# Pacing a batch's loads on the compute of an earlier batch, in a banded attention with a SiLU feed-forward layer

## The chip, the cores and the metric

The kernel runs on one core of a Trainium2 chip. The metric is device time in microseconds (us) of one execution. Lower is better.

## The reference

The kernel computes attention in a causal window of 64 positions, then two dense layers with SiLU between them. Cut to what matters:

```python
# q, k, v: (8 batches, 8 heads, 576 positions, 64), float32
rel = pos[:, None] - pos[None, :]
mask = (rel >= 0) & (rel < 64)
scores = where(mask, (q @ k.T) / sqrt(64), -1e9)
attn = softmax(scores)
x = (attn @ v).transpose(0, 2, 1, 3).reshape(8 * 576, 512)
h = x @ w_in                       # w_in: 512 x 2048
out = (h * sigmoid(h)) @ w_out     # w_out: 2048 x 512, float32 out: 4608 x 512
```

## The kernel before

**The work.** Attention goes by batch: eight of them, each with nine blocks of 64 positions. From batch 2 on, a batch is done in three groups g of three blocks; a group's scores are 24 small matmuls (`scores`, L353), followed by four exponentials on ScalarE (`expo`, L367), four mask products on VectorE (`masking`, L370), 24 matmuls with V (`values`, L376), two reciprocals of the row sums (`inverse`, L383) and two products that normalise (`normal`, L389). The result of a group is turned and written to the tile `bridge`: by TensorE (L393, L404) in the early groups, and by a DMA transpose that SyncE issues (`turn_o`, L398) from the last group of batch 2 on.

The dense part goes by tiles of 512 rows, nine of them, numbered j from 0. A tile's first layer is 64 matmuls (`first_layer`, L409) with 16 SiLUs (L415); its second layer is four times 16 matmuls (`second_layer`, L418), each sixteen copied out of PSUM (`copy_out`, L424, on VectorE or ScalarE) and stored by SyncE (`store`, L428). A tile can begin when the groups of attention that its rows come from are in `bridge`. The attention of later batches is put between the second-layer matmuls of earlier tiles.

**The loads.** Q, K and V of a batch are loaded and cast to bf16 by DMAs that GpSimd issues. From batch 4 on for Q (2 for K), a batch's Q and K come in 16 loads (`load_rows`, L262) into four of the eight buffers `nat0` to `nat7`; each buffer holds two pairs of heads, filled by four loads. Then one DMA transpose for each buffer, issued by SyncE (`turn_rows`, L268), writes it into `qt` or `kt`, of which there are two each, used by batches in turn. So a batch has four such transposes: Q and K of its first half, then Q and K of its second half. V comes in four loads (`load_v`, L276) into one of three buffers `vv`, and two copies on VectorE (`shift_v`, L336 and L338) shift it into place.

**The order.** Each engine runs its instructions in the order in which they were written out. That order comes from a planner in the kernel's own code (`Plan.run`), which walks through time with an estimated cost for each operation (the number in `{"POOL": 0.72}` and the like) and an estimated delay for each DMA, and gives a free engine the ready operation of the highest rank. The estimates decide the order alone; on the chip an instruction starts when its engine gets to it and the semaphores of the data it needs have been raised. GpSimd's loads also wait each for the landing of the load eight before it, as eight semaphores are used in turn; SyncE's DMAs do the same.

Around the change: in the planner, the loads of a batch b from 2 on are held until a planned time, by

```python
hold = {b: p.later(31.0 * b - 31.0 * LEAD) for b in range(2, B)}   # LEAD = 1.5
...
[nat_free.get(i)], dma=0.5, gate=late(b), lat=MARGIN
```

This hold exists in the planner's clock only. On the chip nothing holds the loads but their buffers (`nat_free`: the buffer's last transpose; for V the last use of `vv`) and the eight semaphores.

Of the kernel before, what the change touches and what calls it, by code (L numbers as in the profile page):

```python
# [14 lines left out]
class Plan:  # L15
# [5 lines left out]
    def __init__(self, pools, rank, rank0, ahead):  # L21
        self.rank, self.rank0, self.pools = rank, {**rank0, **{c + "0": r for c, r in ahead.items()}}, pools
        self.queues = {}
        self.banks = [[] for _ in range(8)]
        self.count, self.times = 0, []
        self.now = 0.0

    def add(self, cls, us, fn, deps=(), lat=0.08, gate=None, dma=None, pool=None, table=None, b=0, nb=1):
# [4 lines left out]
        self.count += 1  # L33
        self.queues.setdefault(cls, []).append(op)
        return op

    def later(self, us):
        self.times.append(us)
        return lambda: self.now >= us

    def add_filler(self, n, cls, us, fn, *args, **kw):

# [8 lines left out]
    def run(self):  # L51
        head = {c: 0 for c in self.queues}
        engines = sorted({e for q in self.queues.values() for op in q for e in op["us"]})
        free = {e: 0.0 for e in engines}
        can = {e: [c for c, q in self.queues.items() if any(e in op["us"] for op in q)] for e in engines}
        table, left = "exp", self.count
        pipe, sent = {True: 1.8, False: 0.0}, []
        events, order = [0.0, *self.times], []
        while left:
            if not events:  # L60
                raise RuntimeError([(c, head[c], q[head[c]]["n"]) for c, q in self.queues.items() if head[c] < len(q)])
            now = self.now = heapq.heappop(events)
            while events and events[0] == now:
                heapq.heappop(events)
            moved = True
            while moved:
                moved = False
                for e in engines:
                    if free[e] > now:
                        continue  # L70
                    best, kept = None, set()
                    heads = [(self.queues[c][head[c]], c) for c in can[e] if head[c] < len(self.queues[c])]
                    for op, c in sorted(heads, key=lambda x: x[0]["first"]):
                        if e == "POOL" and op["dma"] and len(sent) >= 8 and sent[-8] > now:
                            continue
                        if e not in op["us"] or not self.done(op["deps"]) or (op["gate"] and not op["gate"]()):
                            continue
                        if op["pool"]:
                            idle = [i for i in self.pools[op["pool"]] if i not in kept and self.done(self.banks[i])]
                            if len(idle) < len(op["untils"]):  # L80
                                if op["pool"] != "mp":
                                    kept.update(self.pools[op["pool"]])
                                continue
                            idle.sort(key=lambda i: (op["pool"] == "mp" and i in self.pools["pv"],
                                                     max([u["seen"] for u in self.banks[i]], default=0.0)))
                            op["bank"] = idle[:len(op["untils"])]
                            for i, until in zip(op["bank"], op["untils"]):
                                self.banks[i] = until
                        best = (op, c)
                        break  # L90
                    if best is None:
                        continue
                    op, c = best
                    head[c] += 1
                    us = op["us"][e]
                    if op["table"] and op["table"] != table:
                        table, us = op["table"], us + 1.28
                    end = free[e] = now + us
                    soft = e == "POOL"
                    if op["dma"] is None:  # L100
                        op["seen"] = end + op["lat"]
                    elif soft:

                        begin = max(pipe[True], end + 1.4)
                        pipe[True] = begin + op["dma"] * (1.5 if pipe[False] > begin else 1.0)
                        op["seen"] = pipe[True] + op["lat"] + (1.2 if now < 40 else 3.2)
                        sent.append(op["seen"])
                        heapq.heappush(events, op["seen"])
                    else:
                        begin = max(pipe[False], end + 1.0)  # L110
                        busy = pipe[True] > begin
                        pipe[False] = begin + op["dma"] * (1.6 if busy else 1.0)
                        if busy:
                            pipe[True] += 0.6 * op["dma"]
                        op["seen"] = pipe[False] + {"ld0": 1.2, "st": 1.2}.get(c, 3.0)
                    op["at"], op["cls"], op["by"] = now, c, e
                    order.append((op, e))
                    left -= c != "warm"
                    moved = True
                    heapq.heappush(events, end)  # L120
                    heapq.heappush(events, op["seen"])
        for op, e in order:
            op["fn"](e)
# [3 lines left out]
def kernel(ctx, tc, q, k, v, w_in, w_out, out):  # L127
# [18 lines left out]
    NXQ, NXK, NXO = 4, 2, 3  # L146
    NOX, NRC, NV = 4, 6, 3
    NIV = 2
    NM0, LEAD, MARGIN = 9, 1.5, 1.3
    scale = 1.0 / float(D) ** 0.5  # L150


# [4 lines left out]

    ident = keep.tile([128, 128], BF16, name="ident")
    zero = keep.tile([128, NP], FP32, name="zero")
    spare = keep.tile([128, NP], FP32, name="spare")  # L160
    window = keep.tile([128, 64], BF16, name="window")
    mask0 = keep.tile([128, 2, 3, 64], BF16, name="mask0")
# [269 lines left out]
    v_landed = {}  # L432
    kq_done, v_done, s_last, pv_last = {}, {}, {}, {}
    nat_free, natb_free = {}, {}
    g_pv, g_norm, g_back, g_mask, o_done = [], [], [], [], {}
    moe = []
    exps = {}

# [9 lines left out]
    scores_may_run.i = 0  # L448

    n_nat = [0, 0]  # L450
    hold = {b: p.later(31.0 * b - 31.0 * LEAD) for b in range(2, B)}

    def late(b):
        return hold.get(b)

    def add_first_batch():
        got = {}
        for what, u in FIRST_LOADS:
# [32 lines left out]
    def add_batch_qk(b):  # L491
        pool = "mp" if b == 3 else "at"
        slot, parts = {}, {0: [], 1: []}
        for pj in range(NP):
            kq_done[(b, pj)] = []
        for pj in range(NP):
            busy = s_last.get((b - NK, pj), []) + ([c_k[b % NK]] if b < NK else [])
            for kk in range(2):
                if b >= (NXK if kk else NXQ):
                    if pj % 2 == 0:  # L500
                        slot[kk] = n_nat[0] % NN
                        n_nat[0] += 1
                    i = slot[kk]
                    parts[kk] += [p.add("dma", {"POOL": 0.72}, lambda _, i=i, pj=pj, kk=kk, hh=hh: load_rows(i, b, pj, kk, hh),
                                        [nat_free.get(i)], dma=0.5, gate=late(b), lat=MARGIN) for hh in range(2)]
                    if pj % 2 == 0:
                        continue
                    both = busy + s_last.get((b - NK, pj - 1), [])
                    done = [p.add("xk", {"SP": 1.4}, lambda _, i=i, pj=pj, kk=kk: turn_rows(i, place(b, pj - 1, kk)),
                                  parts[kk] + both, dma=2.2)]  # L510
                    nat_free[i] = done[0]
                    parts[kk] = []
                    for x in (pj - 1, pj):
                        kq_done[(b, x)] += done
                    continue
                w = n_nat[1] % NNB
                n_nat[1] += 1
                ca = [p.add("dma", {"POOL": 0.66}, lambda _, w=w, pj=pj, kk=kk: load_cast(w, b, pj, kk),
                            [natb_free.get(w)], dma=0.65, gate=late(b), lat=MARGIN)]
                tu = p.add("turn", {"PE": 0.27}, None, ca + [c_ident], lat=0.1, pool=pool, b=b)  # L520
                tu["fn"] = lambda _, tu=tu, w=w: turn_twos(tu, w)
                li = []
# [10 lines left out]

    def add_v_loads(b, parts, busy):
        v_landed.setdefault(b, []).extend(
            p.add("dma", {"POOL": 1.0}, lambda e, part=part: load_v(e, b, part), busy, dma=1.1, gate=late(b), lat=MARGIN * (b > 0)) for part in parts)

    def add_batch_v(b):
        busy = pv_last.get(b - NV, []) + [c_vv[b % NV]]
# [9 lines left out]
    def add_batch_attention(b):  # L549
        pv_last[b] = []  # L550
        whole = b > 1
        for g, a in [(g, a) for a in range(2) for g in range(NG)] if b == 0 else [(g, a) for g in range(NG) for a in range(1 if whole else 2)]:
            add_unit(b, g, range(2) if whole else [a], len(g_pv))

    def add_unit(b, g, which, n0):
# [38 lines left out]
        for i, (n, a) in enumerate(zip(ns, which)):  # L594
            rc = p.add("inverse" + first, {"DVE": 0.21}, lambda _, i=i, n=n: inverse(pv["bank"][i], n),
                       [pv] + g_norm[n - NRC:n - NRC + 1] * (n >= NRC), b=b)
            was = n // 2 - NOX
            no = p.add("norm" + first, {"DVE": 0.56}, lambda e, i=i, n=n: normal(e, pv["bank"][i], n),
                       [rc] + (g_back[2 * was:2 * was + 2] if was >= 0 else []), b=b)
# [128 lines left out]
```

## Time and profile before

| | |
|---|---|
| median of 13 runs | 312.89 us |
| lowest, highest | 309.11, 315.83 us |
| the profiled execution | 314.45 us |
| its span, first to last instruction | 312.7 us |
| TensorE (PE) busy | 296.9 us, 95% |
| ScalarE (ACT), GpSimd (POOL), VectorE (DVE) busy | 185.0, 117.7, 102.2 us |
| first batch-4 load, first batch-5, -6, -7 load issued | 70.14, 89.86, 112.88, 138.35 us |
| last load issued | 160.30 us |
| K or Q transposes, issue to landing | 3.3 to 11.8 us, median 9.1 (K) and 8.7 (Q) |

How to read what follows: the profile is one execution. Engines are PE (TensorE matmuls), PEld (its weight loads), DVE, ACT, POOL and SP (SyncE); a q after the name (SPq) is the engine's sequencer, which issues DMAs and waits. "out<-in" gives the tiles written and read, with buffer numbers left out. Times are microseconds from the start of the span. The "chain" is the work that ended last, followed back step by step to what released it: its rows are start, duration, what. In a timeline a row is start, duration, engine, line, operation, tiles, count, and in brackets the idle time of the engine before it with what ended that.

### The profile page before, as it was taken

The numbers are of one execution on the slowest core, as the hardware profiler recorded it, in microseconds if no ns is written. First come the engines' busy times: TensorE is split into PE (matmuls) and PEld (weight loads), VectorE is DVE, ScalarE is ACT, GpSimd is POOL, SyncE is SP. The second block draws the span as 40 slices with busy tenths as digits, with TensorE's granted clock in tenths as the row PEclk, the third lists the DMA queues.
The fourth block names the chain that finished last, engine by engine and source line by source line (L and its number), as shares of the span: only waits on it lengthen the run. The fifth ranks groups of instructions, "written<-read, shape, count | busy, mean of one in ns | idle before, by whom it ended". The sixth has DMA issues, their size and how long they took to land.

```text
span 312.7 us, 6586 instructions
## 1 busy us (share of the span) xinstructions
PE 296.9 (95%) x2645; PEld 147.6 (47%) x2675; DVE 102.2 (33%) x273; ACT 185.0 (59%) x340; POOL 117.7 (38%) x159
## 2 busy tenths in 40 slices
PE   4999989999999999995999999999999999999995
PEld 2565445445454455442454455445444444444444
DVE  2573877725682066204361056103301200000000
ACT  4788986879466762874328742855478156316611
POOL 8957859866896482773760000000000000000000
PEclk9999999999999999998699999999999999999999
DMA  8999999999999999999999607901400410010012
GB/s 171 162 197 186 193 194 145 186 208 148 189 144 168 120 169 168 157 175 126 171 145 195 101 36 179 150 0 69 107 11 2 93 69 1 34 68 35 0 67 69
DMA packets 137599, 37.57 MB, mean 120 GB/s; under 512 B 122464, under 2 KB 132832, under 8 KB 137568
## 3 DMA queue, kind: packets, MB, share of 16 engines
q0 software_dynamic: 95328, 18.06, 78.8%
q1 hardware_dynamic: 42240, 19.08, 32.7%
q8 instruction: 21, 0.34, 0.5%
q14 instruction: 10, 0.08, 0.1%
HBM read 36.70 MB, written 9.44 MB: 148 GB/s over the span
## 4 chain that ended last, share of the span: by engine, by line
PE 86%; DMA 5%; DVE 3%; issue 2%; ACT 2%; POOL 1%; SPq 0%; POOLq 0%; ACTq 0%
PE mp L409 38%; PE mp L418 37%; DMA kt<-nat 3%; PE mp L376 3%; PE at L353 3%; DMA nat<-in_k_dram 2%; ACT g L415 1%; PE at L313 1%; PE at L303 1%; PE at L376 1%; PE at L673 1%; DVE kt L322 1%; POOL natb L249 1%; PE mp L673 1%; PE at L393 0%
## 5 line engine op out<-in xcount | busy, mean ns | idle before, releaser
L418 PE MATMUL mp<-w_out_sb,g 128*128 128x512 bf16 (+2 forms) x578 | 132.2, 373 | 3.1 <-issue 2.1
L409 PE MATMUL mp<-bridge,w_in_sb 128*128 128x512 bf16 (+2 forms) x600 | 129.4, 370 | 0.3
L415 ACT ACTIVATE g<-mp 128x512 bf16<-128x512 f32 (+2 forms) x150 | 85.3, 580 | 30.1 <-PE mp L409 28.9
L409 PEld LDWEIGHTS <-w_in_sb 128*128 128x128 bf16 x600 | 57.3, 97 | 66.1 <-issue 6.0
L418 PEld LDWEIGHTS <-g 128*128 128x128 bf16 x608 | 55.9, 99 | 59.5 <-issue 3.3
L367 ACT ACTIVATE e<-at 128x384 bf16<-128x384 f32 x88 | 36.8, 496 | 25.1 <-PE at L353 24.6
L424 ACT COPY ot<-mp 128x512 f32<-128x512 f32 (+2 forms) x28 | 15.5, 556 | 58.4 <-PE mp L418 44.9
L370 DVE TENSOR_TENSOR e<-e,mask 128x384 bf16<-128x384 bf16 x84 | 27.0, 353 | 68.8 <-ACT e L367 68.2
L262 POOL DMA_DIRECT2D nat<-in_k_dram x48 | 35.6, 745 | 19.5 <-DMA nat<-in_k_dram 10.1
L276 POOL DMA_DIRECT2D vv<-in_v_dram x32 | 32.1, 1011 | 5.3 <-DMA natb<-in_q_dram 1.5
L262 POOL DMA_DIRECT2D nat<-in_q_dram x32 | 23.7, 745 | 9.4 <-DMA vv<-in_v_dram 5.4
L389 DVE TENSOR_TENSOR ox<-mp,rc 128x384 bf16<-128x384 f32 x37 | 18.5, 537 | 0.0
L376 PEld LDWEIGHTS <-e 128*64 128x64 bf16 x576 | 11.5, 110 | 10.3 <-issue 8.3
L353 PE MATMUL at<-qt,kt 64*128 64x64 bf16 x528 | 13.1, 192 | 3.5 <-DMA kt<-nat 3.3
L353 PEld LDWEIGHTS <-kt 64*128 64x128 bf16 x576 | 10.2, 95 | 11.6 <-issue 7.2
L383 DVE RECIPROCAL rc<-mp 128x6 f32<-128x6 f32 x37 | 7.0, 195 | 21.5 <-PE mp L376 21.4
L424 DVE COPY ot<-mp 128x512 f32<-128x512 f32 x10 | 6.8, 691 | 20.5 <-PE mp L418 19.2
L376 PE MATMUL mp<-vv,e 128*64 128x65 bf16 x444 | 10.8, 196 | 0.2
L322 DVE COPY qt<-at 64x288 bf16<-64x288 bf16 x16 | 7.7, 479 | 7.5 <-ACT qt L322 7.1
L243 POOL DMA_DIRECT2D natb<-in_q_dram x12 | 7.9, 657 | 4.8 <-PE at L313 1.2
L338 DVE COPY vv<-vv 64x576 bf16<-64x576 bf16 (+1 forms) x14 | 8.0, 568 | 3.6 <-issue 2.1
L367 ACT ACT_TABLE_LOAD x7 | 9.0, 1283 | 0.1
(62 smaller groups left out, 137.8 us busy)
## 6 DMA issues: line engine op xcount, KB each, us to landing
out_dram<-ot SPq DMA_DIRECT2D x35, 256.0 KB, 3.7
vv<-in_v_dram POOLq DMA_DIRECT2D x32, 144.0 KB, 7.7
nat<-in_k_dram POOLq DMA_DIRECT2D x48, 72.0 KB, 7.5
nat<-in_q_dram POOLq DMA_DIRECT2D x32, 72.0 KB, 8.4
natb<-in_q_dram POOLq DMA_DIRECT2D x15, 144.0 KB, 6.1
w_in_sb<-in_moe_w_in_dram POOLq DMA_DIRECT2D x8, 256.0 KB, 8.3
w_out_sb<-in_moe_w_out_dram POOLq DMA_DIRECT2D x8, 256.0 KB, 7.4
natb<-in_k_dram POOLq DMA_DIRECT2D x7, 144.0 KB, 5.9
```

Of the source, the lines that this page charges most:

```text
L262: nc.gpsimd.dma_start(out=rows(i)[:, pj % 2, :, 64 * hh:64 * hh + 64], in_=(q, k)[kk][b, head(pj, hh)].rearrange("(m p) d -> p m d", p=NR),)
L276: queue[e].dma_start(out=vv[b % NV][:, 2 * g0 + 1:2 * g1 + 1:2, 0:D], in_=v[b].rearrange("h s d -> (h s) d").rearrange("(g p) d -> p g d", ...
L322: copies[e](out=place_one(b, pj, kk)[64 * hh:64 * hh + 64].rearrange("x (p m) -> x p m", m=NM)[:, :, r::2], in_=at_bf16(op)[64 * r:64 * r ...
L353: nc.tensor.matmul(at_six(of[hh])[:, j, x], lhsT=kt[b % NK][r, at:at + 128], rhs=qt[b % NK][r, at:at + 64], start=(b > 0 and j == x == 0), ...
L367: nc.scalar.activation(out=es[n % NE], in_=at_six(bank), func=ACTF.Exp, scale=scale)
L370: nc.vector.tensor_mul(es[n % NE], es[n % NE], mask0 if g == 0 else mask)
L376: nc.tensor.matmul(at_pv(bank)[64 * hh:64 * hh + 64, j, x], lhsT=es[(2 * n + hh) % NE][:, j, x], rhs=vv[b % NV][:, head(2 * a + j, hh) * N ...
L389: nc.vector.tensor_mul(ox(n), at_pv(bank)[:, :, :, 0:D], rcs[n % NRC].unsqueeze(3).to_broadcast([128, 2, 3, D]))
L409: nc.tensor.matmul(banks[bank["bank"][0]][:, lo:hi], lhsT=w_in_sb[:, c, ft * 128:(ft + 1) * 128], rhs=bridge[:, (j * TT + lo) // 64:(j * T ...
L415: nc.scalar.activation(out=gts[gt][:, lo:hi], in_=banks[bank["bank"][0]][:, lo:hi], func=ACTF.Silu)
L418: nc.tensor.matmul(banks[bank["bank"][0]][:, 0:hi - lo], lhsT=gts[gt][:, m * 128:(m + 1) * 128], rhs=w_out_sb[:, f, lo:hi], start=(f == 0) ...
L424: copies[e](out=ots[ot][:, lo:hi], in_=banks[bank["bank"][0]][:, 0:hi - lo])
```

## The change

The planner's hold goes. In its place the loads of each batch b from 4 on wait on the chip: ahead of them GpSimd runs a copy of one column of the first reciprocal of batch b - 2 into a tile `pace` that nothing reads. GpSimd takes its instructions in order, so all the loads after the copy wait for that reciprocal. The planner sees the copy and its dependency like any other operation.

```diff
-    def later(self, us):
-        self.times.append(us)
-        return lambda: self.now >= us
...
-    NM0, LEAD, MARGIN = 9, 1.5, 1.3
+    NM0, MARGIN, PACED, BEHIND = 9, 1.3, 4, 2
...
+    pace = keep.tile([128, 1], FP32, name="pace")
...
-    hold = {b: p.later(31.0 * b - 31.0 * LEAD) for b in range(2, B)}
-
-    def late(b):
-        return hold.get(b)
...
     def add_batch_qk(b):
         pool = "mp" if b == 3 else "at"
         slot, parts = {}, {0: [], 1: []}
+        if b >= PACED:
+            n = first_unit[b - BEHIND]
+            p.add("dma", {"POOL": 0.15}, lambda _: nc.gpsimd.tensor_copy(out=pace, in_=rcs[n % NRC][:, 0, 0:1]), [g_inverse[n]])
...
-                                        [nat_free.get(i)], dma=0.5, gate=late(b), lat=MARGIN) for hh in range(2)]
+                                        [nat_free.get(i)], dma=0.5, lat=MARGIN) for hh in range(2)]
...
     def add_batch_attention(b):
         pv_last[b] = []
         whole = b > 1
+        first_unit[b] = len(g_pv)
...
             rc = p.add("inverse" + first, {"DVE": 0.21}, lambda _, i=i, n=n: inverse(pv["bank"][i], n),
                        [pv] + g_norm[n - NRC:n - NRC + 1] * (n >= NRC), b=b)
+            g_inverse.append(rc)
```

(`gate=late(b)` goes in the same way from the cast loads and from `load_v`.)

As the planner now sees other load times, it writes out another order. In the built programs:

- GpSimd: the same order, with one copy ahead of the 16 Q/K loads of batches 4, 5, 6 and 7.
- TensorE: the same until the first layer of tile 4. Then batch 6's scores begin at once instead of after 12 second-layer matmuls of tile 4; batch 7's first group moves from tile 5 to tile 4, its second and third groups from tiles 5 and 6 to tile 5.
- VectorE: the two V shifts of batch 4 move from behind batch 3's first group to behind the masks of its second and third group; those of batch 7 move from behind batch 6's third group to behind the masks of its second and third. Four copies out of PSUM move to ScalarE, which has two table loads fewer.
- SyncE: from batch 4 on, as this table shows (Qn.h and Kn.h: transposes of batch n, half h; On.g: turned output of batch n, group g; S: a store).

| | SyncE's order |
|---|---|
| before | O2.2, Q4.0, S, K4.0, O3.0, Q4.1, K4.1, S, O3.1, S, O3.2, O4.0, S, Q5.0, K5.0, S, O4.1, Q5.1, K5.1, S, O4.2, S, O5.0, Q6.0, S, O5.1, K6.0, S, O5.2, Q6.1, K6.1, S, S, O6.0, Q7.0, S, O6.1, K7.0, S, O6.2, Q7.1, K7.1 |
| after | O2.2, S, Q4.0, O3.0, K4.0, Q4.1, K4.1, S, O3.1, S, Q5.0, O3.2, K5.0, O4.0, S, S, O4.1, Q5.1, K5.1, Q6.0, K6.0, S, O4.2, S, Q6.1, O5.0, K6.1, O5.1, S, S, O5.2, Q7.0, K7.0, Q7.1, K7.1, S, O6.0 |

## Prediction

> **What bounds the kernel now.** I read the first part of the page, then the chain of waits between 134 and 165 us, TensorE's timeline there, the stretches with their granted clock, and last the DMA issues and SyncE's timeline.
>
> ```profile
> span 312.7 us, 6586 instructions
> PE 296.9 (95%) x2645; PEld 147.6 (47%) x2675; DVE 102.2 (33%) x273; ACT 185.0 (59%) x340; POOL 117.7 (38%) x159
> ...
> DMA  8999999999999999999999607901400410010012
> ```
>
> TensorE is the bound: 95% busy. A change gains only where TensorE stands idle or runs at a lower clock. The DMA engines are full until about 172 us (22 slices of 7.8 us), while TensorE needs its last batch only at 212 us.
>
> ```profile
> 136.39 0.67 SPq L268
> ...
> 137.26 10.50 DMA kt<-nat
> 147.76 0.05 issue
> 147.81 0.50 PE at L353 x9
> 148.31 0.34 issue
> 148.65 5.23 PE mp L418 x12
> ...
> 154.99 2.75 PE mp L418 x12
> ```
>
> This is the one place after 50 us where the chain leaves TensorE for long: the last K transpose of batch 5, issued by SyncE at 137.26, lands 10.50 us later. TensorE's timeline has the same stop (a row in brackets gives the idle time and who ended it), and the stretches show what follows it:
>
> ```profile
> 144.15 0.35 PE L353 MATMUL at<-qt,kt 64*128 64x64 bf16 x12
> 147.81 0.50 PE L353 MATMUL at<-qt,kt 64*128 64x64 bf16 x12 [3.31 <-DMA kt<-nat]
> ```
> ```profile
> 145.00:146.80 1.80, 0.00 (x0) 0.00 (x0) 0.92 (x3) 0.40 (x2) 0.00 (x0) 1.00 2.02 59
> 146.80:148.00 1.20, 0.19 (x8) 0.19 (x10) 0.00 (x0) 0.00 (x0) 0.19 (x1) 0.51 3.20 109
> 148.00:153.60 5.60, 5.26 (x24) 1.95 (x19) 0.72 (x2) 0.87 (x2) 4.26 (x7) 0.50 2.21 172
> ```
>
> The seventh number column, ahead of DMA share and GB/s, is the granted clock: 1.00 until 146.8, then 0.50 until 153.6. So the stop costs 3.31 us of idle, 0.18 us more issue time (0.34 against 0.16 at the next switch) and 2.48 us of half clock (12 recorded matmuls in 5.23 us against 2.75). Sum 5.97 us. The half clock begins 2.3 us after the idle time does (144.50 to 146.8).
>
> Why did that transpose come so late? Its loads were issued by 108.1 us (GpSimd's timeline) and landed by 115.3. It stood in SyncE's queue:
>
> ```profile
> 103.95 5.30 SPq L268 DMA_TRANSPOSE kt<-nat  x1
> ...
> 116.11 0.34 SPq L428 DMA_DIRECT2D out_dram<-ot  x1
> 117.11 5.08 SPq L398 DMA_TRANSPOSE bridge<-ox  x2
> 122.28 0.56 SPq L428 DMA_DIRECT2D out_dram<-ot  x1
> 123.05 3.88 SPq L268 DMA_TRANSPOSE qt<-nat  x1
> 127.11 3.33 SPq L268 DMA_TRANSPOSE kt<-nat  x1
> ```
>
> Batch 5's first Q transpose, with its data there since about 103 us, waits behind turned outputs and a store that wait for compute. Each transpose then takes long beside loads. Three K transposes, issued at 103.95, 137.26 and 193.22 us, by the DMA issues of windows that hold just these (last number: us to landing):
>
> ```profile
> kt<-nat SPq DMA_TRANSPOSE x1, 11.3
> ```
> ```profile
> kt<-nat SPq DMA_TRANSPOSE x1, 10.5
> ```
> ```profile
> kt<-nat SPq DMA_TRANSPOSE x1, 3.3
> ```
>
> The third ran when no load was left. The first is batch 4's last: it landed at 115.23, and TensorE's scores of batch 4 began at 115.85, their second half at about 116.1. That is a margin of 0.9 us.
>
> **The four copies.** A copy of 128x1 on GpSimd is not in the trace; the nearest GpSimd rows are a 128x1 memset (0.09 us) and a 128x128 select (0.29 us). Four cost 0.4 to 1.2 us of GpSimd, an engine 38% busy and off the chain; they cannot gain by themselves. I take 0.2 each, beside TensorE's work. What they cost is the wait. Behind each stand, on GpSimd, all 20 loads of its batch and of every later one; for them wait SyncE's transposes, for these the scores.
>
> **When the loads now run.** Batch 4: before from 70.14; now after the first reciprocal of batch 2 (VectorE, 82.97 plus 0.2) and the copy: 83.4. Its 16 Q/K loads took 15.4 us before and take 11.6 if nothing but the issue time counts (16 times 0.725); I take 13, as few transposes run beside them: until 96.4. V adds 4.2: 100.6. Batch 5: the reciprocal of batch 3 is done at 92.9, so the copy waits for nothing; loads start at 100.6 (before 89.86), at the old 18.2 + 4.3 us until 123.1. Batch 6: reciprocal of batch 4 at 119.8, also past; 123.1 (before 112.88), 20.2 + 4.2, until 147.5. Batch 7: reciprocal of batch 5, 154.23 less the gain, about 149: a wait of some 1.5 us, then 19.0 + 4.0, until 172. So the loads run 10 to 13 us later, and only batch 4's wait is a real one.
>
> **The queue order.** Until batch 5's scores TensorE's order is unchanged; SyncE's is not. Batch 4: a store and one turned output now stand ahead of its transposes. The store's copy ends at 92.8 (92.10 + 0.69), so the store goes by 93.5 and the first Q transpose at 93.5 instead of 91.10; its loads (the sixth issued at about 87.4, landing in 5) are there. With the old durations (2.75, 3.01, 2.17, 3.12 and four gaps of 0.15) the last K transpose starts at 105.2, against 103.95; the sixteenth load, issued by 96.4 and landing in 5.6 to 9.6, is there by then. Landing after 11.3: 116.5. Needed at 116.1: a wait of 0.4 us. The bounds are a landing 3 us earlier, thus 0, and 2.5 us later, which is past 2.3 us of idle and brings 2.5 us of half clock.
>
> Batch 5: first Q and K move ahead of two turned outputs and two stores. From 116.6 with the old durations: Q 3.88, turned output 1.88, K 3.33, turned output 1.22, two stores 1.1, turned output 2.28, Q 3.40, eight gaps of 0.15: the last K starts at 134.9 instead of 137.26. Loads do not hold it: the sixth lands at about 113.3, the eighth at 117.9, the sixteenth at 126.1 (old times plus 10.8). Plus 10.5 it lands at 145.4; needed at 144.5 plus the 0.4 of batch 4. About 0.7 us of idle remains, too short for the half clock. Bounds: the rows of K transposes beside loads spread from 9.3 to 11.8 us to landing, and one SyncE issue from 2.2 to 5.3: 0 to 3 us, with 2.5 more past 2.3.
>
> Batch 6: two transposes now stand right behind, held until batch 4's last scores (139.4) and their loads (the eighth lands at about 142.6). Behind them waits a store whose copy is ready at 143.7 and a turned output whose norms end at 145.4, needed by a tile that starts 45 us later: nothing.
>
> **The rest of the replan.** The two 0.76 us V shifts of batch 4 on VectorE move behind masks, into idle time shown ahead of reciprocals (0.98 and 1.40): nothing. Four copies out of PSUM move from VectorE to ScalarE (4 times 0.56) while two table loads (1.28 each) go: nothing, as ScalarE is 59% busy; without that cover, one second layer's 3.46 us for 16 matmuls must hold four exponentials (1.64) and a copy (0.59), which it does. Batch 7's first scores come much earlier, at about 186 instead of 212: behind the first layer of tile 4 (172.6) and 13.4 us of other work. Its last K transpose starts at about 173 and lands in 4 to 10: 177 to 183. V lands at 178 to 182, while its shift stands on VectorE at about 181, ahead of a reciprocal and four masks: 0, with 1.5 as the upper bound.
>
> **The sum.** The profiled execution took 314.45 us, 1.75 more than its span, and 1.56 more than the median of 312.89, so the usual stop is likely a shorter one than this one. 314.45 - 5.97 + 0.4 + 0.7 = 309.6 us. Without any wait it is 308.5; the fastest run before was 309.11, so such a floor is near what this kernel already reached.
>
> [...] In the trace 3.31 us of idle were followed by 6.8 us at 0.50. [...] Transposes landed in 10.5 us beside loads and 3.3 without. [...]
>
> **The rivals.**
> *Batch 4 comes late (slower).* Its margin was 0.9 us and its loads start 13 us later. For it: landings of 11.3 us. Against: SyncE's own queue, not the loads, set the old start. It decides when the last K transpose lands after 119.6, that is, starts after 108.3: 3.5 us idle and 2.5 of half clock give back the 5.97, so 314.5, and 315.2 with batch 5's 0.7.
> *No gain.* Batch 5's last transpose still lands over 2.3 us late, as loads crowd it as before. 2.5 idle and 2.5 of clock: 308.5 + 5.0 = 313.5.
> *Real relief.* The late loads leave the transposes room and both waits vanish: 308.5. For it: the 3.3 us row; against: the load queue is dry only from 69.5 to 83.4, before any of these transposes.
> *The change does less than it says:* three of four copies hold nothing. That is in my forecast already.
>
> **How the numbers follow.** About 0.5% (1.6 us) is what a measurement here can tell from no change. Forecast (308.9 to 311.3) 0.47; relief 0.17; no gain (311.3 to 314.45) 0.17; batch 4 late (above that) 0.19. Faster: 0.64, same 0.17, slower 0.19. The range goes from 308.2, just under the floor, to 315.2, the slower rival with both waits.
>
> **What would show it.** Right: GpSimd idle from 69.5 to about 83 and hardly before batches 5 and 6; batch 5's last K transpose issued near 135; no stretch at 0.50 near 147. Wrong: TensorE idle on a transpose at 116, or at 186, or a granted clock of 0.50 anywhere between 60 and 300.

## The result and the profile after

The changed kernel is slower: 320.38 us (median of 11 runs, 316.69 to 322.54) beside 313.15 us for the kernel before on the same chips, a ratio of 1.0227 with a 95% interval of 1.0197 to 1.0256. Medians take in all executions; ratios leave out those that took over 1.5% longer than the fastest of the same kernel. The profiled execution took 322.54 us, the longest of the eleven; its span is 320.4 us.

The page of the changed kernel answers to the one of before:

```profile
span 320.4 us, 6596 instructions
PE 297.0 (93%) x2645; PEld 148.2 (46%) x2675; DVE 99.2 (31%) x269; ACT 184.9 (58%) x342; POOL 118.5 (37%) x163
...
PEclk9999999999999999999999965999999999999999
DMA  8999999999599999999999995200400120020012
```

TensorE's busy time is the same, 297.0 us against 296.9. The extra 7.7 us of span are idle time, and slices 24 and 25 (8 us each) show a fallen clock. Slice 11 of the DMA row, 80 to 88 us, has a hole that was not there before. TensorE's timeline at the stop that the change was forecast to remove, and at the one that came:

```profile
144.20 0.35 PE L350 MATMUL at<-qt,kt 64*128 64x64 bf16 x12
144.96 0.35 PE L350 MATMUL at<-qt,kt 64*128 64x64 bf16 x12 [0.41 <-DMA kt<-nat]
...
181.52 2.97 PE L415 MATMUL mp<-w_out_sb,g 128*128 128x512 bf16 x13 [0.16 <-issue]
194.63 1.35 PE L373 MATMUL mp<-vv,e 128*64 128x65 bf16 x24 [10.15 <-DVE e L367]
195.91 0.82 PE L350 MATMUL at<-qt,kt 64*128 64x64 bf16 x24
197.06 5.39 PE L415 MATMUL mp<-w_out_sb,g 128*128 128x512 bf16 x15 [0.34 <-issue]
```

(Lines here stand three lower than before: L415 is the second layer, L373 the product with V, L367 the mask, L335 one V shift.) Batch 5's stop of 5.97 us is down to 0.41. At 184.5 TensorE then stands still for 10.15 us, and what follows runs slowly. The stretches have the granted clock in the third column from the end:

```profile
184.50:187.40 2.90, 0.00 (x0) 0.00 (x0) 0.00 (x0) 0.00 (x0) 0.00 (x0) 1.00 3.62 121
187.40:194.60 7.20, 0.00 (x0) 0.00 (x0) 2.29 (x7) 0.00 (x0) 0.00 (x0) 0.50 1.44 214
194.60:201.00 6.40, 6.03 (x58) 3.19 (x60) 4.08 (x12) 2.24 (x5) 0.00 (x0) 0.50 0.46 105
```

Against rows of the same kind at full clock (0.57, 0.52, and 2.97 us for 13 matmuls) the work after 194.6 lost 0.8 + 0.3 + 2.0 us, and 0.2 at the switch: 3.2 us. The books close: 312.7 - 5.97 + 0.41 + 10.15 + 3.2 = 320.5, against a span of 320.4.

Who holds TensorE is in the chain of waits:

```profile
152.83 13.00 DMA nat<-in_q_dram
165.83 0.28 issue
166.12 11.45 DMA nat<-in_q_dram
...
181.04 11.11 DMA vv<-in_v_dram
192.15 0.03 issue
192.18 0.05 DVEq L335
...
192.27 0.12 DVE vv L335
...
194.31 0.28 DVE e L367
```

Read backwards: the product with V waits for a mask, the mask stands on VectorE behind a shift of V of batch 7, and that V lands at 192.15. Its last load was issued at 181.04, because loads of batch 7 had waited, through the eight semaphores, for loads that took 13.00 and 11.45 us: the ninth, at 166.12, for the first, which landed at 165.83, and the first V load for the ninth, which landed at 177.56. Before the change, batch 7's first load went out at 138.35 and its last V landed at 171.8; now the first goes out at 152.83, so 14.5 of the 20.3 us come from the later start and the rest from slower loads. The product that stands still belongs to batch 6; it needs nothing of batch 7. Batch 7's last K transpose was no earlier: SyncE issued it at 186.36 and it landed at 192.9.

GpSimd's timeline shows the copies, L488, and the loads behind them:

```profile
83.29 0.18 POOL L488 COPY pace<-rc 128x1 f32<-128x1 f32 x1 [13.93 <-DVE rc L380]
...
100.15 0.22 POOL L488 COPY pace<-rc 128x1 f32<-128x1 f32 x1
...
152.72 0.22 POOL L488 COPY pace<-rc 128x1 f32<-128x1 f32 x1
...
157.88 0.72 POOL L259 DMA_DIRECT2D nat<-in_q_dram  x1 [1.17 <-DMA vv<-in_v_dram]
162.95 0.72 POOL L259 DMA_DIRECT2D nat<-in_k_dram  x1 [4.34 <-DMA vv<-in_v_dram]
```

Only the first copy waited for its reciprocal, 13.93 us. The others ran as soon as GpSimd came to them.

### The profile page after: what moved, and what is told of

Its sections match the earlier page's. It is cut to its first block, busy times and chain, and to the rows that moved or that the text cites. A ratio compares the mean times of both kernels' runs of the same rounds, so it can differ in the third digit from the quotient of the medians.

```text
span 320.4 us, 6596 instructions
## 1 busy us (share of the span) xinstructions
PE 297.0 (93%) x2645; PEld 148.2 (46%) x2675; DVE 99.2 (31%) x269; ACT 184.9 (58%) x342; POOL 118.5 (37%) x163
## 4 chain that ended last, share of the span: by engine, by line
PE 69%; DMA 23%; POOL 3%; issue 3%; DVE 1%; POOLq 0%; SPq 0%; ACT 0%; DVEq 0%; ACTq 0%
PE mp L415 31%; PE mp L406 29%; DMA nat<-in_q_dram 8%; DMA natb<-in_q_dram 5%; DMA vv<-in_v_dram 3%; DMA kt<-nat 3%; DMA w_out_sb<-in_moe_w_out_dram 3%; PE mp L373 2%; PE at L350 2%; POOL vv L273 2%; DMA nat<-in_k_dram 1%; POOL w_out_sb L285 1%; PE at L300 1%; PE at L373 1%; PE mp L670 1%
## 5 line engine op out<-in xcount | busy, mean ns | idle before, releaser
L415 PE MATMUL mp<-w_out_sb,g 128*128 128x512 bf16 (+2 forms) x578 | 131.2, 372 | 3.2 <-issue 2.2
L415 PEld LDWEIGHTS <-g 128*128 128x128 bf16 x608 | 55.8, 99 | 59.4 <-issue 3.2
L421 ACT COPY ot<-mp 128x512 f32<-128x512 f32 (+2 forms) x32 | 17.8, 560 | 62.8 <-PE mp L415 47.4
L367 DVE TENSOR_TENSOR e<-e,mask 128x384 bf16<-128x384 bf16 x84 | 27.1, 353 | 44.9 <-ACT e L364 44.1
L259 POOL DMA_DIRECT2D nat<-in_q_dram x32 | 23.8, 749 | 12.7 <-DMA vv<-in_v_dram 8.4
L373 PEld LDWEIGHTS <-e 128*64 128x64 bf16 x576 | 12.0, 112 | 20.5 <-DVE e L367 11.9
L373 PE MATMUL mp<-vv,e 128*64 128x65 bf16 x444 | 11.6, 199 | 10.3 <-DVE e L367 10.1
L335 DVE COPY vv<-vv 64x576 bf16<-64x576 bf16 (+1 forms) x14 | 8.3, 591 | 36.5 <-DMA vv<-in_v_dram 29.8
L380 DVE RECIPROCAL rc<-mp 128x6 f32<-128x6 f32 x37 | 6.3, 188 | 15.4 <-PE mp L373 13.7
L319 ACT COPY qt<-at 64x288 bf16<-64x288 bf16 x16 | 7.6, 476 | 0.7 <-DVE qt L319 0.2
L310 PEld LDWEIGHTS <-natb 96*128 96x128 bf16 x96 | 5.7, 97 | 4.7 <-issue 1.8
```

Of the source, the lines that this page charges most:

```text
L259: nc.gpsimd.dma_start(out=rows(i)[:, pj % 2, :, 64 * hh:64 * hh + 64], in_=(q, k)[kk][b, head(pj, hh)].rearrange("(m p) d -> p m d", p=NR),)
L319: copies[e](out=place_one(b, pj, kk)[64 * hh:64 * hh + 64].rearrange("x (p m) -> x p m", m=NM)[:, :, r::2], in_=at_bf16(op)[64 * r:64 * r ...
L367: nc.vector.tensor_mul(es[n % NE], es[n % NE], mask0 if g == 0 else mask)
L373: nc.tensor.matmul(at_pv(bank)[64 * hh:64 * hh + 64, j, x], lhsT=es[(2 * n + hh) % NE][:, j, x], rhs=vv[b % NV][:, head(2 * a + j, hh) * N ...
L415: nc.tensor.matmul(banks[bank["bank"][0]][:, 0:hi - lo], lhsT=gts[gt][:, m * 128:(m + 1) * 128], rhs=w_out_sb[:, f, lo:hi], start=(f == 0) ...
L421: copies[e](out=ots[ot][:, lo:hi], in_=banks[bank["bank"][0]][:, 0:hi - lo])
```

## The experiments

The change does two things: it makes loads wait on the chip, and it writes out another order. The first four runs take them apart. My theory A was that the order gains and batch 4's wait, through the lateness of batch 7's data, loses. The rivals are in each expectation. Twelve further kernels were run; ratios are to the kernel before, with 95% intervals.

| run | waits of batches | order | us | ratio |
|---|---|---|---|---|
| the change | 4, 5, 6, 7 | new | 320.4 | 1.023 [1.020, 1.026] |
| e1 order alone | none | new | 312.8 | 0.998 [0.994, 1.002] |
| e2 wait alone | 4, 5, 6, 7 | old | 318.7 | 1.019 [1.014, 1.024] |
| e3 shift back | 4, 5, 6, 7 | new, V shift later | 317.7 | 1.015 [1.009, 1.022] |
| e4 only first waits | 4 | new | 320.3 | 1.025 [1.020, 1.030] |
| e5 first free | 5, 6, 7 | new | 308.7 | 0.989 [0.984, 0.995] |
| e6 b7 later | 4, 5, 6, 7 | new, b7 scores later | 318.9 | 1.021 [1.016, 1.026] |
| e7 both later | 4, 5, 6, 7 | new, both later | 310.3 | 0.994 [0.990, 0.998] |
| e8 both, no wait | none | new, both later | 309.8 | 0.991 [0.988, 0.994] |
| e9 free, both later | 5, 6, 7 | new, both later | 308.1 | 0.986 [0.981, 0.991] |
| e10 half wait | 4 for 6 us; 5, 6, 7 | new | 312.8 | two groups, see below |
| e11 old order, first free | 5, 6, 7 | old | 311.8 | 0.996 [0.993, 0.999] |
| e12 most wait | 4 for 10.5 us; 5, 6, 7 | new | 318.2 | 1.017 [1.011, 1.024] |

### The order without the waits (e1)

```diff
-  ...tensor_copy(out=pace, in_=rcs[n % NRC][:, 0, 0:1]), [g_inverse[n]])
+  ...tensor_copy(out=pace, in_=zero[:, 0:1]), [g_inverse[n]])
```

The planner still sees the dependency, so the order on every engine is that of the changed kernel; on the chip the copy reads a constant.

> The changed kernel with the same order on every engine, but its four GpSimd copies read a tile that is ready from the start, so no load waits for compute. Theory A (the waits make batch 7's V and last K land at about 192, and the new order wants them at 181 and 185): without the waits batch 7's V is issued by about 161 and lands by 172 as before; no stop of TensorE at 184, batch 5's last K transpose still issued near 135, so 308.5 to 310.5 us, faster than both kernels. Theory B (only the place of batch 7's V shift in VectorE's queue is at fault): the same, as V is early. Theory C (the new order of SyncE's queue makes the transposes and loads collide, wait or no wait): the loads of batch 7 still take 25 us, V lands after 185, 317 to 321 us.

Measured 312.8 us, the same as before. So the waits cost some 7.6 us, as theory A says, but the order alone gains nothing, which theory A did not say. Batch 5's stop is gone (0.41 left) and another has come:

```profile
186.45 1.34 PE L373 MATMUL mp<-vv,e 128*64 128x65 bf16 x24 [2.47 <-DVE e L367]
```

It is the place of the changed kernel's stop. With loads of batch 7 from 139.2, as early as before, its V lands at 184.0 and not at 171.8: its 16 Q/K loads took 23.6 us to issue, against 18.3 before. In the new order batch 6's transposes are issued from 139 to 156 beside these loads; before, from 157 on. GpSimd's idle time between these loads ended with landings of earlier loads. That the transposes are what slowed them is the likeliest reading; no run moves the transposes alone.

### The waits in the old order (e2)

The kernel before, with its planner's hold kept and the copies added; on SyncE and VectorE only batch 4's transposes and V shift change place.

```diff
+        if b >= PACED:
+            n = first_unit[b - BEHIND]
+            p.add("dma", {"POOL": 0.15}, lambda _: nc.gpsimd.tensor_copy(out=pace, in_=rcs[n % NRC][:, 0, 0:1]), [g_inverse[n]])
```

> The kernel before, its planner's hold kept, with the four waiting copies added; only batch 4's first transposes and V shifts move by a place or two, the rest of the order is that of before. Theory A: batch 7's V lands near 190 and its K near 195, but this order wants them at 195 and 212, so there is no stop there; batch 5's last K transpose keeps its old place and lands late as before (TensorE idle 2 to 5 us near 145). 311 to 315 us, within 0.7% of the kernel before. Theory C says the same. A theory that the waits cost in any order, by late loads alone, says 318 to 322 us.

Measured 318.7 us. The rival (318 to 322) was right and theory A (311 to 315) wrong: the old order asks for batch 7 some 25 us later, and yet the waits cost nearly as much, a ratio of 1.019 to the kernel before, beside 0.998 and 1.023 for the new order without and with them. The stops stand elsewhere:

```profile
150.14 0.50 PE L354 MATMUL at<-qt,kt 64*128 64x64 bf16 x12 [4.11 <-DMA kt<-nat]
...
184.11 0.35 PE L354 MATMUL at<-qt,kt 64*128 64x64 bf16 x12 [1.89 <-DMA kt<-nat]
```

These are the scores (L354 in this kernel) of batch 5 and batch 6, held by the last K transpose of each. The late loads were paid here at batches 5 and 6, which are due before batch 7.

### Moving the two things that were late (e3, e6, e7)

e3 puts batch 7's V shifts behind batch 6's last normalisations, e6 puts batch 7's first scores behind 16 second-layer matmuls of tile 5, e7 does both. All keep the four waits.

```diff
-                        lv[a:z], b=b) for hf in range(2)]
+                        lv[a:z] + g_norm[-1:] * (b == 7), b=b) for hf in range(2)]
...
-                  + (g_mask[-1] if b > 1 else []), lat=0.1, ...
+                  + (g_mask[-1] if b > 1 else []) + ([second[5, 16]] if (b, g) == (7, 0) else []), lat=0.1, ...
```

> The changed kernel, waits kept, with batch 7's two V shifts put back behind batch 6's third group on VectorE. Theory B: nothing blocks the masks of batch 6 any more, TensorE runs through, 309 to 311 us. Theory A: the last K transpose of batch 7 still lands near 192, while its scores are due at 186, so TensorE stops there instead: 6 to 8 us idle, then half clock, 317 to 320 us.

> The changed kernel with all its waits; only the scores of batch 7's first group are put back, behind 16 matmuls of the second layer of tile 5 (some 25 us later). Batch 7's V shift stays between the masks of batch 6. Theory A (two things of batch 7 are late, each of them at a place of its own): the last K transpose is no longer waited for, but the V shift still holds VectorE until V lands at about 192; TensorE idles some 8 to 10 us near 185 to 194 and runs 10 to 13.7 us at half clock: 319 to 321 us. Rival (TensorE has enough other work once batch 7 stands later, so the shift's wait is hidden): 309 to 313 us.

> As the run before, and batch 7's V shifts also stand behind the normalisations of batch 6's last group, as in the shift-back run. All four waits are kept, loads as late as in the changed kernel. Theory A (the waits cost only because the new order asks for batch 7 at 181 and 185, before it has landed at 192): no TensorE idle time over 1.5 us between 60 and 280, V and last K landing at about 192 and wanted at 200 or later; 308.5 to 311 us, faster than both kernels. Rival C (late loads cost in any order, as the wait alone in the old order did with 318.7): the stop moves to batch 5 or 6, 314 to 319 us.

e3 took 317.7 us. VectorE is free, and TensorE now waits for the K transpose that lands at 191.1:

```profile
191.11 0.50 PE L350 MATMUL at<-qt,kt 64*128 64x64 bf16 x12 [4.41 <-DMA kt<-nat]
```

e6 took 318.9 us, with the stop at the mask still there (8.0 us). Either half alone brings little, some 2 us in e3, with an interval that overlaps that of the changed kernel, and nothing that can be told in e6, since the other late thing is next. e7, with both, took 310.3 us, though V of batch 7 landed at 190.1 and its last K at 191.0, as late as in the changed kernel. The times are theory A's (e6 0.1 us under its range), but its "no idle time over 1.5 us" for e7 was not: what remains in that profile, of an execution of 312.26 us, is a stop on batch 5, which this move does not touch:

```profile
146.96 0.50 PE L350 MATMUL at<-qt,kt 64*128 64x64 bf16 x12 [2.72 <-DMA kt<-nat]
```

### The same without waits (e8)

e7 with the copies reading a constant, as in e1.

> The order of the run before with all four copies reading a constant, so that nothing waits. Theory A: V of batch 7 lands at about 184 and is wanted later, no stop over 1.5 us; 308.5 to 310.5 us, at most 1 us from the run with the waits. Rival C (the new order on SyncE itself makes loads and transposes collide): 311.5 to 313 us, as the order alone. If this and the run before differ by over 3 us, the waits cost something that is not the wanted time of batch 7.

309.8 us, within what theory A gave, and by the ratios not to be told from e7: once batch 7 is asked for later, the four waits cost little. They may still cost something now and then, since five of e7's twelve executions took over 312 us and none of e8's did; the stop on batch 5, 2.72 us in e7's profile, is 0.44 us in e8's.

### Which copy does it (e4, e5)

e4 lets batch 4's copy alone wait, e5 lets all wait but batch 4's:

```diff
+  ...in_=rcs[n % NRC][:, 0, 0:1] if b == PACED else zero[:, 0:1]), [g_inverse[n]])    # e4
+  ...in_=zero[:, 0:1] if b == PACED else rcs[n % NRC][:, 0, 0:1]), [g_inverse[n]])    # e5
```

> The changed kernel with only batch 4's copy waiting; those of batches 5, 6 and 7 read a tile that is ready. In the changed kernel's trace these three found their reciprocals done when GpSimd came to them. Theory A: nothing changes, batch 7's loads start near 153, 317 to 322 us. A theory that every wait adds its share says in between, 311 to 316 us.

> The changed kernel's order, with batch 4's copy reading a constant, while the copies of batches 5, 6 and 7 still wait for their reciprocals. Theory A (a wait costs what it delays batch 7's data): batch 5 then starts at about 92.9 us (the reciprocal of batch 3), batch 6 is held to 119.8 and batch 7 to about 149, some 4 us earlier than the 152.8 of the changed kernel and 10 us later than the 139.2 of the order alone. Batch 7's V lands at about 188, TensorE stops for 5 to 7 us near 186 and runs 6.8 us at half clock: 315 to 318 us. Rival (batch 4's copy is the whole of it, and the other copies hold nothing once it is free): as the order alone, V at 184, 312 to 313.5 us.

e4 is the changed kernel again, 320.3 us with a stop of 9.03 us: e1 differs from it in batch 4's wait alone and took 312.8, so this wait is the whole loss, as theory A had it. e5 contradicted both theories. I expected 315 to 318 us from batch 7 being held to 148; the rival expected that nothing holds, 312 to 313.5. It took 308.7 us, faster than the kernel before, and its copies did wait:

```profile
92.58 0.18 POOL L488 COPY pace<-rc 128x1 f32<-128x1 f32 x1 [2.14 <-DVE rc L380]
...
119.89 0.18 POOL L488 COPY pace<-rc 128x1 f32<-128x1 f32 x1 [4.61 <-DVE rc L380]
...
147.80 0.18 POOL L488 COPY pace<-rc 128x1 f32<-128x1 f32 x1 [8.17 <-DVE rc L380]
```

That is 14.9 us of holding, more than the 13.93 of the changed kernel, and batch 7's V landed at 180.1 instead of 192.2: earlier than in e1 without any hold (184.0). What counted here is thus first when the loads were held, and only then how long. Behind the last two holds the loads went out fast: batch 6's 16 took 12.7 us (120.4 to 133.1) and batch 7's 13.5 us (148.3 to 161.8), against 23.8 and 23.2 in the changed kernel and 19.2 and 23.6 in e1. TensorE has no idle stretch over 0.3 us between 60 and 280.

The stretches of the two kernels around the first hold say why it is different (last column GB/s); the changed kernel first, then e5:

```profile
70.00:77.50 7.50, 7.44 (x66) 3.66 (x65) 4.03 (x10) 6.74 (x13) 0.00 (x0) 1.00 1.94 153
77.50:84.00 6.50, 6.29 (x94) 3.28 (x95) 4.24 (x12) 4.43 (x11) 0.20 (x2) 1.00 0.27 94
84.00:90.00 6.00, 5.84 (x93) 2.94 (x92) 5.07 (x16) 2.24 (x5) 6.00 (x8) 1.00 1.13 106
```
```profile
70.00:77.50 7.50, 7.50 (x85) 3.71 (x85) 3.93 (x10) 7.06 (x13) 4.36 (x6) 1.00 2.28 151
77.50:84.00 6.50, 6.50 (x90) 3.18 (x81) 4.35 (x14) 3.92 (x10) 4.87 (x7) 1.00 2.08 166
84.00:90.00 6.00, 6.00 (x95) 3.11 (x94) 5.07 (x16) 2.39 (x6) 6.00 (x8) 1.00 1.87 177
```

Until 77.5 both move the same, as batch 3's loads, issued by 69, are still landing. Then the changed kernel's DMA engines have little left. Over 70 to 100 us it moves 133 GB/s against e5's 166, 0.99 MB less; over 100 to 165, 158 against 171, another 0.85 MB. At 158 GB/s these 1.84 MB are 11.6 us; V is 12.1 us later. The same sum for e1 (165 and 161 GB/s, 0.68 MB, 4.2 us) meets 3.9 us. It is a rough sum: for e8, e12 and e7 it gives 7.4, 9.1 and 13.1 us, and their V lands 5.4, 6.6 and 10.0 us later than e5's.

What is missing before 100 us goes with batch 4's hold. Most of what is missing from 100 to 165 us does not, since e1, without any hold, also moves 0.65 MB less there than e5. It is a gain of e5 behind its holds, as in this stretch (the changed kernel, then e5):

```profile
120.40:132.00 11.60, 11.54 (x75) 5.38 (x75) 3.96 (x12) 7.23 (x13) 6.82 (x9) 1.00 2.05 137
```
```profile
120.40:132.00 11.60, 11.60 (x77) 5.32 (x76) 5.32 (x13) 7.11 (x13) 10.50 (x15) 1.00 1.74 195
```

In the holds of e5 the engines had turned outputs, transposes and the last V to move: 186 GB/s from 113.8 to 120.4 and 138 from 138.6 to 148.3. The last V of batches 4, 5 and 6 landed at 96.7, 121.2 and 148.7, each after the hold beside it had ended (92.6, 119.9, 147.8). In the changed kernel batch 3's last V landed at 77.5, and the hold went on until 83.3.

### How much hold is free (e10, e12)

From here on theory E: a hold costs only what it leaves the DMA engines without work. The changed kernel's order is kept, and batch 4's copy reads a masked exponential that is ready earlier than the reciprocal.

```diff
+  ...in_=es[2 * n % NE][:, 0, 0, 0:1] if b == PACED else rcs[n % NRC][:, 0, 0:1]), ...          # e10, ready at 76
+  ...in_=es[(2 * n + 7) % NE][:, 0, 0, 0:1] if b == PACED else rcs[n % NRC][:, 0, 0:1]), ...    # e12, ready at 80
```

> The changed kernel in its own order; only what batch 4's copy reads is another tile, a masked exponential of batch 2's first group that is ready at about 76.1 us, so batch 4 is held 6 us and not 13. Theory D (every microsecond of hold of batch 4 comes out at batch 7): V lands at 186 to 190, TensorE stops 4 to 7 us near 190 and runs 3.4 to 10 us at half clock: 313 to 317 us. Theory E (a hold is free while earlier transfers still keep the DMA engines busy, which is until the last loads of batch 3 land at about 77.5): V lands at 180 to 185, 308 to 311 us.

> As the half-wait run, with a masked exponential of batch 2's second group, ready at about 80.6 us: batch 4 is held 10.5 us of the 13. Theory D: V at 190 to 191, 317 to 319.5 us. Theory E: some 3 us of DMA time are lost between 77.5 and 80.8, V at 184 to 188, TensorE stops 2 to 5 us with 3.4 to 6.8 at half clock: 311 to 316 us.

| batch 4's first load | 70.4 (e5) | 76.5 (e10) | 80.9 (e12) | 84.0 (the change) |
|---|---|---|---|---|
| GB/s, 77.5 to 84 | 166 | 144 | 123 | 94 |
| batch 7's V lands | 180.1 | 183.5 | 186.7 | 192.2 |
| median | 308.7 | 312.8 | 318.2 | 320.4 |

V's landing is what theory E gave (180 to 185, 184 to 188) and not what theory D gave (186 to 190, 190 to 191). The times are above theory E's: e10 was expected at 308 to 311. Its ten runs fall in two groups, three at 308.1 to 308.6 and seven at 311.4 to 315.0, so one ratio says little; the median of the ten, 312.8, is that of the kernel before beside them (313.1). The profiled execution, at 312.88, is of the upper group and shows the edge it stands on:

```profile
185.96 1.18 PE L373 MATMUL mp<-vv,e 128*64 128x65 bf16 x24 [2.31 <-DVE e L367]
```

That is 2.31 us idle and then half clock, at which the next 16 second-layer matmuls took 5.31 us instead of 3.63, about 1.7 more: 4.0 us, about the distance of the groups. e12's profile, of its fastest execution (315.94), has two stops, 2.58 us on batch 5's last K and 2.79 here; its median is 2 us over theory E's range. So a hold of 6 us stands at the edge of what is free, and 10.5 us is past it.

e12 also shows how a hold helps the loads behind it, since its batch 6 starts at the same moment as e5's, 120.4, and takes 22.9 us for 16 loads where e5 takes 12.7:

```profile
119.16 0.99 POOL L273 DMA_DIRECT2D vv<-in_v_dram  x1
120.15 0.20 POOL L488 COPY pace<-rc 128x1 f32<-128x1 f32 x1
...
129.60 0.73 POOL L259 DMA_DIRECT2D nat<-in_q_dram  x1 [4.51 <-DMA vv<-in_v_dram]
```

With no hold between V of batch 5 (issued until 119.2, landing until 132.6) and these loads, most of them wait for the landing of one eight places earlier.

### The holds in the old order, and the best version (e11, e9)

e11 is e2, e9 is e7, each with batch 4's copy reading a constant as in e5.

> The kernel before, in its own order save for batch 4's transposes and V shift, with the holds of batches 5, 6 and 7 alone (batch 4's copy reads a constant). Theory E with the old order: the holds give the transposes room, batch 5's last one is still issued late (near 137) but lands sooner, so part of the old stop of 6 us stays: 309 to 313 us. Rival (the holds alone do the whole work and the order none of it): no stop, 307 to 309 us. Rival (holds cost in the old order, as the four waits did): 315 to 318 us.

> Batch 4's copy reads a constant, the copies of batches 5, 6 and 7 wait, and batch 7's first scores and V shift stand later, as in the two runs of the both-later order. Theory E (a hold costs only where the DMA engines run out of queued work; the holds at 92.6, 119.9 and 147.8 did not): no stop over 1 us between 60 and 280, V of batch 7 landing at 180 to 184, 307.5 to 309.5 us, the same as the first-free run within 0.5%, since that had no stop left either. Rival (a later batch 7 takes work away from under the end of the kernel): 310 to 312 us.

e11 took 311.8 us, within theory E's range and 6.8 us below e2: batch 4's wait costs in the old order too, though less than the 11.7 us between the changed kernel and e5. Its three holds removed batch 5's old stop, and one on batch 6 replaced it:

```profile
176.39 0.35 PE L354 MATMUL at<-qt,kt 64*128 64x64 bf16 x12 [2.23 <-DMA kt<-nat]
```

e5 and e9 with the new order are lower. That the three holds gain, beyond costing nothing, is less sure: the intervals of e5 and e1 only just touch (0.9946 and 0.9944), those of e9 and e8 overlap. e9 took 308.1 us, 1.4% below the kernel before (0.986, 0.981 to 0.991), and no run of it was above 308.33. That is within theory E's range, and its V of batch 7 landed at 181.2, as expected. It beats both kernels. It is not to be told from e5 (308.7).

## Why the prediction was wrong

I predicted 309.6 us, with 0.64 for faster, and the range ended at 315.2.

**What held.** The four copies took 0.18 to 0.23 us each (0.2 put down). Batch 4's Q/K loads ran from 84.0 to 96.0 (83.4 to 96.4), batch 5's from 100.3 with V until 124.1 (100.6, 123.1). Only batch 4's wait was real, and e4 shows it. Batch 4's last K transpose was issued at 105.87 and landed at 115.23 (105.2, 116.5), with no stop; batch 5's at 135.50 and 144.92 (134.9, 145.4), with 0.41 us of idle (0.7; the forecast's own 145.4 less 144.5 and 0.4 is 0.5). So the gain that the forecast rests on came in full: 5.97 - 0.41 = 5.56 us.

**What failed.** One term, in the paragraph on the rest of the replan: "Its last K transpose starts at about 173 and lands in 4 to 10: 177 to 183. V lands at 178 to 182, while its shift stands on VectorE at about 181, ahead of a reciprocal and four masks: 0, with 1.5 as the upper bound." V landed at 192.15, the transpose at 192.9, and the term measured 10.15 us of idle and 3.2 of half clock and switch. The order alone makes 2.47 us of that idle time (e1); the rest came with batch 4's hold. With it in the sum, 314.45 - 5.97 + 0.41 + 13.35 is 322.2, against 322.54 for the profiled execution.

Two things went into it.

First, the load times. I took batches 6 and 7 at their old durations (20.2 + 4.2 and 19.0 + 4.0 us, until 147.5 and 172). They took 28.4 and 29.2 us (124.3 to 152.7, 152.8 to 182.0), and the last V issue ended 10 us later than I had it. Those durations belonged to an order in which batch 7's loads ran with few transposes beside them. I had shown that transposes suffer beside loads (10.5 us to landing against 3.3) and had not asked what loads suffer beside transposes that I was moving forward by 10 to 20 us; e1 shows the slower loads with no wait at all, V at 184.0 instead of 171.8, though no run moves those transposes alone.

Second, I had named the blockade (the shift, "ahead of a reciprocal and four masks") and priced it at 0 to 1.5 us, about the length of the two shifts (0.76 us each). What the shift cost was the lateness of its data, for all that was queued behind it: V landed at 192.15, and the mask that TensorE waited for ended at 194.59. The margin between the forecast landing, 178 to 182, and 181 was nothing, so the error in the loads went into TensorE. Of the signs of being wrong that I had named, the clock of 0.50 came, from 187.4 on; the idle time ahead of it ended with a mask and not with a transpose.

**The rivals.** "Batch 4 comes late" had the right cause, loads 13 us later, and the wrong place: batch 4 itself had no stop, batch 7 paid. "Real relief" put its argument against itself rightly: the load queue ran dry only ahead of batch 4, where no transpose could profit. Holds that fell on a full queue did no harm in e5 (308.7 us), and the transposes and loads around them ran faster there (6.1 and 6.6 us to landing, 12.7 and 13.5 us for 16 loads). "No gain" is refuted at batch 5, and e1 shows how the order alone comes to nothing all the same: the gain there is given back at batch 7. "Three of four copies hold nothing" was right.

**The transposes and the clock.** The first Q and K transposes of batch 5 with the load queue running, in e1, then the same two in e5, Q issued in a hold (at 116.20) and K 0.65 us after loads had begun again (at 121.06; last number: us to landing):

```profile
qt<-nat SPq DMA_TRANSPOSE x1, 10.2
```
```profile
kt<-nat SPq DMA_TRANSPOSE x1, 9.5
```
```profile
qt<-nat SPq DMA_TRANSPOSE x1, 6.1
```
```profile
kt<-nat SPq DMA_TRANSPOSE x1, 6.6
```

This goes the way of the prediction's own rows (10.5 us beside loads, 3.3 without): these two landed sooner in e5, where the load queue moved less beside them (0.05 MB from 116 to 118 us against 0.19 MB in e1). It is not the empty queue of the 3.3 us row, since V of batch 5 was landing in e5 until 121.2; the change had emptied the queue, at the wrong time, ahead of batch 4. On the clock, the prediction took 2.3 us of idle, from one trace, as the length past which half clock follows. The runs draw no such line: it followed stops of 2.23 (e11), 2.31 (e10), 2.47 (e1), 2.72 (e7) and 2.79 us (e12), and did not follow one of 2.58 us (e12) (last section).

## What to carry to other kernels

In these runs a hold on loads was free only while earlier transfers still kept the DMA engines busy: put it where a backlog stands, and look at the GB/s of the stretch that it covers (186 and 138 in the last two holds of e5, at 308.7 us; 94 from 77.5 to 84 in the changed kernel, at 320.4). The DMA time lost in the changed kernel came out at batch 7, whose V landed 12.1 us later than in e5, and was paid because that batch was due before it landed (in e7, where batch 7 was due later, little was paid: 310.3 us). Load durations read from a trace belong to the transfers that ran beside them (batch 7's 16 loads took 18.3 us before and 23.6 in e1); when the order moves these, take them anew. When an instruction that waits for data stands ahead of other work in an engine's order, price it by how late the data may be, not by how long it takes (the V shifts: 0.76 us each, and 10.15 us of idle on TensorE).

## What the runs showed of the hardware

The half-clock stretch between 60 and 300 us lasted 6.8 us before (146.8 to 153.6) and 13.6 us in the changed kernel (187.4 to 201.0). In e1, e7 and e10 the mean clocks (0.91 from 182 to 200; 0.97 from 124 to 148 and 0.94 from 148 to 165; 0.91 from 180 to 200) make it some 3.2, 3.5 and 3.6 us, and in e3 (0.83 from 180 to 200) some 6.8 us: estimates, with the rate of 0.50 that the first two stretches had. e5, e8 and e9 had none (mean clocks of 0.999, 1.000 and 1.000 in the profiled executions).

The stretch did not begin at a fixed idle time: before, it began 2.3 us after TensorE had stopped, in the changed kernel 2.9 us. In e10, where TensorE stopped at 183.65 and went back to work at 185.96, the 24 scores at 187.07 still took 0.52 us, as at full clock, and the 16 second-layer matmuls from 187.53 took 5.31 us instead of 3.63. A stop of 1.89 us (e2) drew none: the 19 second-layer matmuls behind it took 4.28 us. One of 2.23 us (e11) did, 5.96 us for 19. One of 2.58 us (e12, at 146.6) did not, 2.98 us for 13, as elsewhere at full clock.

From the first issue to the last, the same 16 loads took 11.3 us after a dry spell (batch 4 in the changed kernel, 83.98 to 95.30). For batches 6 and 7 they took 12.7 and 13.5 us in e5, behind holds of 4.61 and 8.17 us, and batch 6's took 12.9 in e10, behind 4.61 us. With no hold just ahead of them they took 19.5 and 18.3 us before, 23.8 and 23.2 in the changed kernel, 19.2 and 23.6 in e1, and batch 6's 22.9 in e12. Batch 5's show no such gap between e1, without a hold, and e5, held for 2.14 us: 14.7 and 15.6 us.
